# Keys and values of a cached attention block in mixed rows of 65536 bytes, three loads for two heads

## The chip, the core and the metric

The kernel runs on one core of one Trainium2 chip. The metric is the device time of one execution in microseconds (us). Times below are from one profiled execution, unless a median of runs is named. The engines are called PE (matrix products; PEld is its loading of weights), DVE (vector), ACT (activations), POOL and SP (which issues every load here).

## What is computed

One token passes through a transformer block with adaptive normalisation. All numbers are float32. The attention has 32 heads of width 192 and a cache of 8192 keys and values for each head, so the two caches hold 402.7 MB of the 451.8 MB that the kernel reads.

```python
D = 640; H, Sk, Dh = 32, 8192, 192; F = 1536
mod = (silu(c) @ w_mod).reshape(6, D)            # sa, ca, ga, sb, cb, gb
h = layernorm(x) * (1 + ca) + sa
q = (h @ wq).reshape(H, Dh)
scores = einsum("hd,hkd->hk", q, k_cache) * Dh ** -0.5
p = softmax(scores)
o = einsum("hk,hkd->hd", p, v_cache)
x = x + ga * (o.reshape(H * Dh) @ wo)
h = layernorm(x) * (1 + cb) + sb
x = x + gb * (relu(h @ w1 + b1) ** 2 @ w2 + b2)
```

## The kernel before

**Tiles.** A head's 8192 positions lie on 128 partitions, 64 positions each. A head's keys are therefore one tile of 128 rows of 12288 numbers (49152 bytes), and its values another. There are four large buffers: `k0` and `k1` for the keys of even and odd heads, `v0` and `v1` for their values. A row of `k0` or `k1` has room for 1920 more numbers. With 26 of the 32 heads a piece of a weight is appended to the keys: with an even head the columns of `wq` for the next two heads, with an odd head the rows of `wo` for two earlier heads. Such a row has 14208 numbers (56832 bytes).

**One head.** DVE multiplies the keys in place by the query, which lies in `qb` on all partitions (L368). It sums 36 of the 64 positions over the 192 dimensions (L370). For the other 28, POOL first adds the second half of the dimensions to the first (L347), and DVE sums what is left (L376). Then comes the maximum over the positions: DVE in each partition (L378), PE across partitions, DVE again (L380, negated). ACT forms the exponentials (L315) and PE multiplies them with the values: 24 products, which the profile counts as 48 (L271). For two heads together PE forms the next query from `wq` in `k0` (L283).

**Work that lies inside the next pair.** Between L370 and L376 of an even head, DVE divides the two outputs before by their sums and sorts them (L388, L354, L356). Between L370 and L376 of an odd head it multiplies an earlier pair's outputs with the rows of `wo` that came with the keys and adds them to `acc` (L405, three instructions a pair). For the last five pairs `wo` is loaded after the keys (`wot`), and its products stand behind the loop: three pairs on DVE (L468), two on PE (L489).

**Order of the loads.** SP issues all loads by one function (L135) into one queue. It waits for a buffer to come free before each: `tk_f0` and `tk_f1` say that DVE has finished the keys, a mark of PE that the values were used. Behind the last heads come `wot`, `wm1` (second half of `w_mod`), `w1` and `w2` in four pieces, 73 loads in all.

**The end.** After the last values PE turns the outputs (L288), forms the attention's result (L489, L497), then the second normalisation (L508 to L519), the product with `w1` (L529), squares, and the product with `w2` (L548), whose pieces it waits for one by one.

```python
    def dma(dst, src, s):
        nc.sync.dma_start(dst, src).then_inc(s, 16)
```

Of the kernel before, what the change touches and what calls it, by code (L numbers as in the profile page):

```python
# [9 lines left out]
P = 128  # L10
# [16 lines left out]
HALF = NPOS // 2  # L27
FOLD = 7
WO = 3 * D
WQ = KB * PW  # L30
HD = NPOS * DH
KSLOT = HD + WO
NTAIL = 4
WITHOUT_W = (1, H - 2, *range(H + 1 - 2 * NTAIL, H, 2))
WITH_W = tuple(h for h in range(H) if h not in WITHOUT_W)
SMALL = 2 * KB + FB + KB
W0 = KB * 3 * D + WQ + SMALL
W2_CUT = (6 * D, 9 * D, 11 * D, FB * D)
EPS = 1e-5
# [52 lines left out]
def block_kernel(nc, kw, ky, vc, wm0, wot, wm1, w1, w2, out):  # L92
# [4 lines left out]
    k0_sem = sem("k_first")  # L97
    k_sem = [sem(f"k{s}") for s in range(2)]
    b_sem = [sem(f"v{s}") for s in range(2)]
    w_sem = [sem(f"w{n}") for n in range(9)]  # L100
    me, tk_mul, tk_n = sem("me"), sem("tk_mul"), sem("tk_n")
    tk_free = [sem("tk_f0"), sem("tk_f1")]
    tk_fold, tk_qb, tk_v, tk_x, tk_t = sem("tk_fold"), sem("tk_qb"), sem("tk_v"), sem("tk_x"), sem("tk_t")
    tk_q, tk_m, tk_o = sem("tk_q"), sem("tk_m"), sem("tk_o")
# [9 lines left out]

    k_t = [sb(f"k{s}", KSLOT) for s in range(2)]
    v_t = [sb(f"v{s}", HD) for s in range(2)]
# [3 lines left out]
    qb, ga, x_t, bbt = sb("qb", PW), sb("ga", DG), sb("x_t", DG), sb("bbt", 32 * (FB + KB))  # L120
# [4 lines left out]
    sp = sb("sp", 2)  # L125
    r2 = sb("r", 2)
    om, os_ = sb("om", ED, E), sb("os", 2, ED)
    oT, oTs, acc = sb("oT", 1 + NTAIL, NV), sb("oTs", NV), sb("acc", D)
# [8 lines left out]
    dma(v_t[1][:, :W0], wm0, w_sem[0])  # L137

    def keys_of(h):
        return kw[WITH_W.index(h)] if h in WITH_W else ky[WITHOUT_W.index(h)]  # L140
# [15 lines left out]
    pool.memset(eps_t[:, :], EPS)  # L156
    m_quad = L.mark(pool.memset(quad[:, :], 0.0))
# [5 lines left out]
    L.e.wait_ge(*m_set).then_inc(tk_o, 1)  # L163
# [3 lines left out]
    head = v_t[1][:, W0:]  # L167
# [5 lines left out]
    m_small = V.mark(v.tensor_copy(small[:, :], v_t[1][:, W0 - SMALL:W0]))  # L173
# [47 lines left out]
    m_mod = mod(ps_o[0], v_t[1][:, :KB * 3 * D], 3, range(KB))  # L221
# [16 lines left out]
    T.wait(m_h1)  # L238
    wq0 = v_t[1][:, KB * 3 * D:KB * 3 * D + WQ].rearrange("p (b n) -> p b n", b=KB)
    for b in range(KB):  # L240
        i = pe.matmul(ps_q[:, :PW], h1[:, b:b + 1].to_broadcast([P, P]), wq0[:, b], start=(b == 0), stop=(b == KB - 1))
    m_q = T.mark(i)
# [12 lines left out]


    PE_STEPS = ("q", "oT", "v0", "sum", "v1")
# [4 lines left out]
    T0 = T.n  # L262

    def pe_values(s):
        T.take(b_sem[s], 16)
        T.take(tk_p[s])
        t = v_t[s][:, :].rearrange("p (j g n) -> p j g n", g=NV, n=E * ED)
        n = NPOS // E
        for j in range(n):
            for g in range(NV):  # L270
                i = pe.matmul(ps_o[s][32 * g:32 * (g + 1), :], p_t[s][:, E * j:E * (j + 1)].rearrange("p e r -> p (e r)"),  # L271
                              t[:, j, g], start=(j == 0), stop=(j == n - 1))
        i.then_inc(T.sem, 1)
# [16 lines left out]
    def pe_sum():  # L290
# [27 lines left out]
    late, turned_to = NPAIR - 1 - NTAIL, {}
    act_query(0, m_q)
    for i in range(NPAIR):  # L320
        if i:
            A.wait(done("oT", i))
            turned = act.activation(oTs[:, :] if i <= late else oT[:, i - 1 - late], ps_oT[:, :NV], AF.Copy)  # L323
            if i <= late:
                turned.then_inc(tk_t, 1)
            else:
                turned_to[i - 1] = A.mark(turned)
        act_exp(2 * i)
        if i + 1 < NPAIR:
# [28 lines left out]
    def dve_keys(h, between):  # L358
        s = h % 2
        for n, (a, b) in enumerate(parts(h)):  # L360
            if h == 0 and n == 0:
                V.wait((k0_sem, 16))
            else:
                B.take(k_sem[s], 16)
            if s == 0 and n == 0:
                B.take(tk_qb)
            pr, r, keep = keys(s, a, b), sc[s][:, a:b], b - a - FOLD * (b - a) // 16
            B.mark(v.tensor_mul(pr, pr, qb[:, None, DH * s:DH * (s + 1)].to_broadcast([P, b - a, DH])))  # L368
            B.tell(tk_mul)
# [12 lines left out]
    def dve_pair(i, projected, attended):  # L382

        def even():
            if not projected:
                return
# [12 lines left out]
        def odd():  # L399
            if attended:  # L400
                B.take(tk_t)
                w = k_t[1][:, HD:].rearrange("p (j n) -> p j n", j=NV)
                for j in range(NV):
                    B.wait()
                    B.mark(v.scalar_tensor_tensor(acc[:, :], w[:, j], oTs[:, j:j + 1], acc[:, :], op0=ALU.mult, op1=ALU.add))  # L405

        dve_keys(2 * i, even)
        dve_keys(2 * i + 1, odd)
# [3 lines left out]
    dve_pair(0, False, False)  # L412
    for first, end, attended in ((1, late + 1, True), (late + 1, NPAIR, False)):
        with nc.Fori(first, end, engines=bass.OrderedEngineSet([ET.DVE])):
            dve_pair(first, True, attended)


    S.wait(m_q, m_h1, m_ready)
    def load_values(h):
        if h > 1:  # L420
            S.wait(done(f"v{h % 2}", h // 2 - 1))
        dma(v_t[h % 2][:, :], vc[h], b_sem[h % 2])

    def load_keys(h):
        S.wait((tk_free[h % 2], h // 2))
        if h % 2 == 0:
            S.wait(done("q", h // 2 - 1))
        w = KSLOT if h in WITH_W else HD
        dma(k_t[h % 2][:, :w], keys_of(h), k_sem[h % 2])

    for h in range(1, H - 2):
        load_values(h)
        load_keys(h + 1)
# [165 lines left out]
```

## Time and profile before

| what | before |
|---|---|
| median of 3 runs | 1052.62 us (1052.47 to 1052.73) |
| the profiled execution | 1052.46 us |
| its span, first to last instruction | 1051.2 us |
| bytes loaded | 451.8 MB |
| mean rate over the span | 430 GB/s |
| DMA queue's packets, share of 16 engines | 99.6% |
| DVE busy | 852.9 us, 81% |
| PE busy | 412.2 us, 39% |
| POOL busy, ACT busy | 190.1 us, 35.7 us |

The span is 1.26 us shorter than the execution's time. An engine's busy time says only how long it worked. Which resource sets the time is read from the share of the DMA engines, from the waits, and from the chain that ended last.

### The profile page before, as it was taken

How to read it: one execution, taken by the hardware profiler on the slowest of the kernel's cores; microseconds unless marked ns; L12 is line 12 of the kernel's file. 1: busy time of each engine (PE TensorE's matmuls, PEld its weight loads, DVE VectorE, ACT ScalarE, POOL GpSimd, SP SyncE). 2: the span in 40 equal slices, each digit the busy share in tenths (PEclk: the TensorE clock that was granted, in tenths of full speed). 3: DMA queues.
4: the chain of work that ended last, by engine and by line, in shares of the span. 5: the costliest groups of instructions: out<-in, count | busy, mean ns of one | idle time of the engine just before them, and what ended most of it. 6: DMA issues, size and time to landing. Idle time of an engine off the chain costs nothing. (4 is left out here: it accounts for less than half of the span.)

```text
span 1051.2 us, 5316 instructions
## 1 busy us (share of the span) xinstructions
PE 412.2 (39%) x2128; PEld 157.2 (15%) x2128; DVE 852.9 (81%) x327; ACT 35.7 (3%) x103; POOL 190.1 (18%) x48
## 2 busy tenths in 40 slices
PE   2153514344341444424234441433424334353447
PEld 0021201112110111201012110111201111121213
DVE  0976889888889888889888888888889889797983
ACT  1000000000000000000000000000000000000000
POOL 0110222201222210222210222220122222012220
PEclk9676657768566676757767576676756667676669
DMA  9999999999999999999999999999999999999998
GB/s 401 429 451 424 427 430 446 425 436 438 432 428 426 443 441 421 428 445 433 428 434 438 429 428 428 443 438 423 437 434 426 445 428 437 429 428 434 434 427 342
DMA packets 10526, 451.90 MB, mean 430 GB/s; under 512 B 1172, under 2 KB 1176, under 8 KB 1560
## 3 DMA queue, kind: packets, MB, share of 16 engines
q1 hardware_dynamic: 10520, 451.83, 99.6%
q8 instruction: 3, 0.05, 0.0%
q14 instruction: 3, 0.02, 0.0%
HBM read 451.82 MB, written 0.00 MB: 430 GB/s over the span
## 5 line engine op out<-in xcount | busy, mean ns | idle before, releaser
L368 DVE TENSOR_TENSOR k<-k,qb 128x12288 f32<-128x12288 f32 (+1 forms) x33 | 414.8, 12570 | 109.5 <-DVEq L75 109.5
L347 POOL TENSOR_TENSOR k<-k 128x2688 f32<-128x2688 f32 (+1 forms) x33 | 188.1, 5699 | 819.2 <-DVEq L85 819.2
L271 PE MATMUL ps_o<-v,p 128*32 128x512 f32 x1536 | 264.6, 675 | 22.0 <-PEq L57 22.0
L370 DVE TENSOR_REDUCE sc<-k 128x36 f32<-128x6912 f32 (+1 forms) x33 | 235.5, 7135 | 4.8
L283 PE MATMUL ps_q<-k,h 128*128 128x384 f32 x160 | 91.0, 743 | 242.3 <-PEq L57 242.3
L277 PE MATMUL ps_mx<-ident,mp 128*128 128x128 f32 x64 | 19.6, 399 | 326.9 <-PEq L57 326.7
L271 PEld LDWEIGHTS ps_o<-v,p 128*32 128x32 f32 x1536 | 71.5, 122 | 189.4 <-issue 189.1
L376 DVE TENSOR_REDUCE sc<-k 128x28 f32<-128x2688 f32 (+1 forms) x33 | 94.3, 2857 | 0.0
L283 PEld LDWEIGHTS ps_q<-k,h 128*128 128x128 f32 x160 | 46.4, 302 | 290.7 <-issue 287.6
L277 PEld LDWEIGHTS ps_mx<-ident,mp 128*128 128x128 f32 x64 | 12.8, 249 | 341.7 <-issue 341.6
L380 DVE TENSOR_REDUCE nm<-ps_mx 128x1 f32<-128x128 f32 x32 | 9.3, 292 | 33.9 <-DVEq L75 33.9
L405 DVE SCALAR_TENSOR_TENSOR acc<-k,oTs,acc 128x640 f32<-128x640 f32 x33 | 29.1, 882 | 0.8
L315 ACT ACTIVATE p<-sc,nm 128x256 f32<-128x256 f32 x32 | 16.2, 507 | 275.2 <-DVE nm L380 275.2
L354 DVE SCALAR_TENSOR_TENSOR om<-ps_o,r,mask 96x512 f32<-96x512 f32 x32 | 23.9, 746 | 1.1
L356 DVE TENSOR_REDUCE os<-om 96x64 f32<-96x512 f32 x32 | 21.8, 682 | 1.1
L292 PE MATMUL ps_sum<-sp,ones 128*128 128x2 f32 x32 | 8.9, 348 | 20.5 <-PEq L57 20.5
L310 ACT ACTIVATE qb<-ps_q 128x384 f32<-128x384 f32 x16 | 7.9, 491 | 231.6 <-DVEq L85 226.9
L188 PE MATMUL ps_o<-v,silu 128*32 128x480 f32 x40 | 6.4, 804 | 18.4 <-DVE silu L181 18.4
L323 ACT ACTIVATE oTs<-ps_oT 128x3 f32<-128x3 f32 x11 | 1.9, 173 | 328.5 <-PE ps_oT L288 328.5
L292 PEld LDWEIGHTS ps_sum<-sp,ones 128*128 128x128 f32 x32 | 8.0, 311 | 24.8 <-issue 24.8
L173 DVE COPY small<-v 128x27 f32<-128x27 f32 x1 | 0.2, 180 | 14.0 <-DMA v<-in_wm 14.0
L378 DVE TENSOR_REDUCE mp<-sc 128x1 f32<-128x64 f32 x32 | 7.0, 220 | 4.7
(88 smaller groups left out, 84.4 us busy)
## 6 DMA issues: line engine op xcount, KB each, us to landing
v<-in_vc SPq DMA_DIRECT2D x32, 6144.0 KB, 39.4
k<-in_kw SPq DMA_DIRECT2D x25, 7104.0 KB, 35.9
k<-in_ky SPq DMA_DIRECT2D x6, 6144.0 KB, 35.5
v<-in_wm SPq DMA_DIRECT2D x1, 5773.5 KB, 16.6
k<-in_wot SPq DMA_DIRECT2D x1, 4800.0 KB, 28.2
v<-in_wm SPq DMA_DIRECT2D x1, 4800.0 KB, 28.6
k<-in_kw SPq DMA_DIRECT2D x1, 4032.0 KB, 33.3
k<-in_w SPq DMA_DIRECT2D x1, 3840.0 KB, 24.1
```

Source lines behind the costliest of these rows:

```text
L271: i = pe.matmul(ps_o[s][32 * g:32 * (g + 1), :], p_t[s][:, E * j:E * (j + 1)].rearrange("p e r -> p (e r)"), t[:, j, g], start=(j == 0), s ...
L277: pe.matmul(ps_mx[s][:, :P], mp[s][:, :].to_broadcast([P, P]), ident[:, :], start=True, stop=True).then_inc(tk_x, 1)
L283: i = pe.matmul(ps_q[:, :PW], h1[:, b:b + 1].to_broadcast([P, P]), w[:, b], start=(b == 0), stop=(b == KB - 1))
L292: pe.matmul(ps_sum[:, :2], ones[:, :], sp[:, :], start=True, stop=True).then_inc(T.sem, 1)
L315: act.activation(p_t[s][:, :, :], sc[s][:, :, None].to_broadcast([P, NPOS, 32 // E]), AF.Exp, bias=nm[s][:, :], accum_out=sp[:, s:s + 1]). ...
L347: pool.tensor_add(half[:, :, :DH // 2], half[:, :, :DH // 2], half[:, :, DH // 2:]).then_inc(tk_fold, 1)
L354: return (v.scalar_tensor_tensor(om[:n], ps_o[a][:n].rearrange("p (d e) -> p d e", e=E), r2[:n, a:a + 1], mask[:n, None, :].to_broadcast([ ...
L356: lambda: v.tensor_reduce(os_[:n, a], om[:n], axis=AX.X, op=ALU.add))
L368: B.mark(v.tensor_mul(pr, pr, qb[:, None, DH * s:DH * (s + 1)].to_broadcast([P, b - a, DH])))
L370: o = v.tensor_reduce(r[:, :keep], pr[:, :keep], axis=AX.X, op=ALU.add)
L376: B.mark(v.tensor_reduce(r[:, keep:], pr[:, keep:, :DH // 2], axis=AX.X, op=ALU.add))
L405: B.mark(v.scalar_tensor_tensor(acc[:, :], w[:, j], oTs[:, j:j + 1], acc[:, :], op0=ALU.mult, op1=ALU.add))
```

## The change

**Loads.** The four buffers become a ring of three slots of 16384 numbers (65536 bytes) a partition. The first half of a slot holds keys, the second half values. A pair of heads is cut into three chunks. The keys are cut by dimension: dimensions 0 to 127 of the even head; 128 to 191 of the even and 0 to 63 of the odd head; 64 to 191 of the odd head. The values of a pair are cut into three runs of 16 products. Chunk n goes to slot n mod 3, and carries the keys of chunk n and the values of chunk n - 2. There are 48 chunks of keys; loads 48 and 49 (`c48`, `c49`) carry the last values and, in the place of the keys, rows of `wo`.

**Queries.** All of `wq` comes in the first four loads (`l0`, `l1`, `c0`, `c1`). PE computes all queries at once into `qr`, five rounds of up to four pairs (`query_rows`). In the loop ACT picks a pair's row (`act_stage`) and PE copies it to all partitions (`pe_query`, one product instead of five).

**Output weights.** No rows of `wo` come with the keys. They come last: four pairs with `c48`, eight in a load `wos`, four with `c49`. The products of pairs 0 to 13 stand on DVE behind the loop, those of 14 and 15 on PE.

**DVE.** A chunk has one multiplication, two sums and POOL's fold, over 8192 numbers instead of 12288. The two parts of a head's scores are added by one small instruction (L413). SP waits for each landing and passes it on by `tk_k` to DVE and `tk_c` to PE. There are 59 loads.

```diff
-    dma(v_t[1][:, :W0], wm0, w_sem[0])
-    dma(k_t[0][:, :HD // 2], keys_of(0)[:, :HD // 2], k0_sem)
-    dma(k_t[0][:, HD // 2:], keys_of(0)[:, HD // 2:], k_sem[0])
-    dma(k_t[1][:, :HD], keys_of(1), k_sem[1])
-    dma(v_t[0][:, :], vc[0], b_sem[0])
+    dma(slot[2][:, :L0], l0, w_sem[0])
+    dma(slot[1][:, :L1], l1, w_sem[1])
+    dma(slot[0][:, :PART + 4 * WQ], c0, slot_sem[0])
...
+    def dve_keys(s, out, between=None):
+        B.take(tk_k)
+        if s == 0:
+            B.take(tk_qb)
...
+        B.mark(v.tensor_mul(k, k, q))
+        B.tell(tk_mul)
+        v.tensor_reduce(out[:, :keep], r[:, :keep], axis=AX.X, op=ALU.add)
+        if between:
+            between()
+        B.take(tk_fold)
+        B.mark(v.tensor_reduce(out[:, keep:], r[:, keep:, :r.shape[2] // 2], axis=AX.X, op=ALU.add))
+        B.tell(tk_free)
+
+    def dve_max(s, one, two):
+        B.mark(v.tensor_add(sc[s][:, :], one, two))
...
+        dve_keys(0, ra)
+        dve_keys(1, rb, between if projected else None)
+        dve_max(0, ra[:, :], rb[:, :NPOS])
+        dve_keys(2, rc)
+        dve_max(1, rc[:, :], rb[:, NPOS:])
...
+    S.wait(m_w1, m_w2)
+    dma(slot[1][:, :PART + WQ], c1, slot_sem[1])
+    S.wait(m_w0, m_h1, m_ready)
+    dma(slot[2], stream[0], slot_sem[2])
+
+    def forward(n):
+        m = landed(n)
+        if n < PARTS:
+            nc.sync.wait_ge(*m).then_inc(tk_k, 1)
+        if n >= LAG:
+            nc.sync.wait_ge(*m).then_inc(tk_c, 1)
...
+    def issue(n):
+        old = n - 3
+        S.wait((tk_free, old + 1))
+        if old >= LAG:
+            S.wait(values_done(old - LAG))
...
+            dma(slot[n % 3], stream[n - LAG], slot_sem[n % 3])
...
+    forward(0)
+    for n in range(1, PARTS - 1):
+        forward(n)
+        issue(n + 2)
+    forward(PARTS - 1)
+    S.wait((tk_free, PARTS), values_done(PARTS - 3))
+    dma(slot[2][:, :MIDDLE * WO], wos, w_sem[2])
+    issue(PARTS + 1)
+    forward(PARTS)
+    forward(PARTS + 1)
+
+    attend_range(0, EARLY, landed(PARTS))
+    attend_range(EARLY, EARLY + MIDDLE, (w_sem[2], 16))
...
+    S.wait(done("vb", NPAIR - 1), attended[EARLY - 1])
+    dma(wm1_t, wm1, w_sem[3])
+    S.wait(attended[EARLY + 3])
+    dma(w1_t, w1, w_sem[4])
+    S.wait(attended[EARLY + MIDDLE - 1])
...
+        "stream": np.concatenate([kp[LAG:], vp[:-LAG]], axis=2),
+        "c48": join(side(wo, 0, EARLY), vp[-2]),
+        "c49": join(side(wo, EARLY + MIDDLE, 4), vp[-1]),
+        "wos": side(wo, EARLY, MIDDLE),
```

SP's queue at the end of the program, before; `k0` to `v1` are the four buffers, `pe` and `tk_f0`, `tk_f1` the marks that a buffer is free:

```order
L135 DMA v0<-in_vc 128x12288 [waits pe]
L135 DMA v1<-in_vc 128x12288 [waits pe]
L135 DMA k0<-in_wot 128x9600 [waits pe,tk_f0]
L135 DMA v0<-in_wm1 128x9600 [waits pe]
L135 DMA k1<-in_w1 128x7680 [waits tk_f1]
L135 DMA v1<-in_w2 128x3840 [waits pe]
```

Now; `slot0` to `slot2` are the landings of loads to the slots, `tk_free` says that DVE has finished a chunk's keys:

```order
L144 DMA ring<-in_stream 128x16384 [waits slot0,pe,tk_free]
L144 DMA ring<-in_c48 128x15872 [waits slot1,pe,tk_free]
L144 DMA ring<-in_wos 128x15360 [waits slot2,pe,tk_free]
L144 DMA ring<-in_c49 128x15872
L144 DMA ring<-in_wm1 128x9600 [waits slot0,slot1,dve,pe]
L144 DMA ring<-in_w1 128x7680 [waits dve]
L144 DMA ring<-in_w2 128x3840 [waits dve]
```

Before, each of these loads waited for an engine to free its buffer. Now `c48` and `wos` wait for an earlier load's landing as well, and SP's waits ahead of `wm1` are for the landings of `c48` (`slot0`) and `c49` (`slot1`), the load issued just before it.

DVE behind its loop, before; `k0` holds `wot`:

```order
L471 RECIPROCAL r<-ps_sum 128x2 [waits pe]
L354 SCALAR_TENSOR_TENSOR om<-ps_o0,r,mask 96x512 [waits dve]
L356 TENSOR_REDUCE os<-om 96x64 [waits dve]
L468 SCALAR_TENSOR_TENSOR acc<-k0,oT,acc 128x640 [waits act,w8,dve]
L468 SCALAR_TENSOR_TENSOR acc<-k0,oT,acc 128x640 [waits dve] x2
```

Now, the first rows of the 36 products with `wo` there, and the rows that stand behind them:

```order
L451 SCALAR_TENSOR_TENSOR acc<-ring,oT,acc 128x640 [waits act,slot0]
L451 SCALAR_TENSOR_TENSOR acc<-ring,oT,acc 128x640 [waits dve] x2
...
L451 SCALAR_TENSOR_TENSOR acc<-ring,oT,acc 128x640 [waits dve,act,w2]
...
L515 RECIPROCAL r<-ps_sum 128x2 [waits pe]
L388 SCALAR_TENSOR_TENSOR om<-ps_o0,r,mask 96x512 [waits pe,dve]
L390 TENSOR_REDUCE os<-om 96x64 [waits dve]
L451 SCALAR_TENSOR_TENSOR acc<-ring,oT,acc 128x640 [waits act,slot1,dve]
```

Behind the loop there were nine products with `wo` on DVE; now there are 42, of which 36 stand ahead of the division of the last pair's outputs, 24 of them behind the landing of `wos` (`w2`).

## Rows read from the trace of the kernel before

**Rows 1.** The page: span; GB/s in 40 equal slices; DMA packets; the load queue.
```profile
span 1051.2 us, 5316 instructions
GB/s 401 429 451 424 427 430 446 425 436 438 432 428 426 443 441 421 428 445 433 428 434 438 429 428 428 443 438 423 437 434 426 445 428 437 429 428 434 434 427 342
q1 hardware_dynamic: 10520, 451.83, 99.6%
```

**Rows 2.** Stretches A:B: length, busy us by engine, clock, DMA share, GB/s.
```profile
502.60:565.30 62.70, 23.01 (x120) 8.84 (x117) 52.90 (x19) 1.86 (x6) 11.75 (x2) 0.70 1.00 433
...
1017.00:1027.40 10.40, 10.26 (x63) 3.17 (x66) 9.14 (x12) 0.00 (x0) 0.00 (x0) 0.72 0.98 421
...
1031.00:1038.90 7.90, 7.31 (x56) 2.13 (x49) 3.70 (x14) 0.47 (x2) 0.00 (x0) 1.00 0.97 418
```

**Rows 3.** DVE's timeline: multiplications of odd heads' keys (start, us, what, idle before).
```profile
471.42 12.96 DVE L368 TENSOR_TENSOR k<-k,qb 128x12288 f32<-128x12288 f32 x1 [3.76 <-DVEq L75]
...
784.64 12.96 DVE L368 TENSOR_TENSOR k<-k,qb 128x12288 f32<-128x12288 f32 x1 [3.75 <-DVEq L75]
...
845.03 12.96 DVE L368 TENSOR_TENSOR k<-k,qb 128x12288 f32<-128x12288 f32 x1 [6.39 <-DVEq L75]
```

**Rows 4.** Timeline of the launch: first load issued, first instruction that needs it.
```profile
0.75 0.40 SPq L135 DMA_DIRECT2D v<-in_wm  x1
...
17.32 0.18 DVE L173 COPY small<-v 128x27 f32<-128x27 f32 x1 [14.04 <-DMA v<-in_wm]
```

**Rows 5.** Groups of instructions by shape (busy, mean ns of one, idle before).
```profile
L368 DVE TENSOR_TENSOR k<-k,qb 128x12288 f32<-128x12288 f32 x31 | 401.7, 12958 | 108.0 <-DVEq L75 108.0
...
L370 DVE TENSOR_REDUCE sc<-k 128x36 f32<-128x6912 f32 x31 | 228.0, 7353 | 4.5
L347 POOL TENSOR_TENSOR k<-k 128x2688 f32<-128x2688 f32 x31 | 182.0, 5871 | 774.8 <-DVEq L85 774.8
...
L368 DVE TENSOR_TENSOR k<-k,qb 128x6144 f32<-128x6144 f32 x2 | 13.1, 6552 | 1.5 <-DVEq L75 1.5
...
L188 PE MATMUL ps_o<-v,silu 128*32 128x480 f32 x40 | 6.4, 804 | 18.4 <-DVE silu L181 18.4
```

**Rows 6.** DVE's timeline through the end of the last even head.
```profile
976.65 7.35 DVE L370 TENSOR_REDUCE sc<-k 128x36 f32<-128x6912 f32 x1
983.92 0.16 DVE L388 RECIPROCAL r<-ps_sum 128x2 f32<-128x2 f32 x1
...
987.00 2.94 DVE L376 TENSOR_REDUCE sc<-k 128x28 f32<-128x2688 f32 x1
990.08 0.22 DVE L378 TENSOR_REDUCE mp<-sc 128x1 f32<-128x64 f32 x1
991.06 0.29 DVE L380 TENSOR_REDUCE nm<-ps_mx 128x1 f32<-128x128 f32 x1 [0.76 <-DVEq L75]
991.27 12.95 DVE L368 TENSOR_TENSOR k<-k,qb 128x12288 f32<-128x12288 f32 x1
```

**Rows 7.** PE's timeline: one head's values.
```profile
960.74 9.09 PE L271 MATMUL ps_o<-v,p 128*32 128x512 f32 x48
```

**Rows 8.** Timeline of the end, several engines.
```profile
1019.44 8.38 DVE L468 SCALAR_TENSOR_TENSOR acc<-k,oT,acc 128x640 f32<-128x640 f32 x9
...
1028.51 0.68 DVE L356 TENSOR_REDUCE os<-om 96x64 f32<-96x512 f32 x1
...
1031.04 0.33 DVE L508 TENSOR_TENSOR k<-ps_att,ga 128x160 f32<-128x160 f32 x1 [1.85 <-PE ps_att L489]
...
1037.38 0.34 DVE L519 STREAM_TRANSPOSE k<-k 128x160 f32<-128x160 f32 x1
...
1038.92 3.43 PE L529 MATMUL ps_o<-k 128*32 128x384 f32 x40 [0.60 <-DMA k<-in_w]
...
1047.34 1.25 PE L548 MATMUL ps_o<-v,k 128*32 128x160 f32 x24 [0.45 <-DMA v<-in_w]
...
1049.37 0.65 SPq L135 DMA_DIRECT2D out_y<-k  x1
```

More of the change, by code (lines that the diff above doesn't have):

```diff
@@ L89, in close, with block_kernel @@
         self.n = 0
-def block_kernel(nc, kw, ky, vc, wm0, wot, wm1, w1, w2, out):
+def block_kernel(nc, l0, l1, c0, c1, stream, c48, c49, wos, wm1, w1, w2, out):
     sem = nc.alloc_semaphore
@@ new lines, in act_stage, with pe_query @@
+    def act_stage(i):
+        r = [i in pairs for pairs in ROUNDS].index(True)
+        g = ROUNDS[r].index(i)
+        A.wait(m_rows[r])
+        return act.activation(stage[:, :], qr[:, r], AF.Copy, scale=ident[:, 32 * g:32 * g + 1])
+    def pe_query():
+        return pe.matmul(ps_q[:, :PW], ones[:, :], stage[:, :], start=True, stop=True)
+    m_rows = {}
+    A.wait(m_set)
+    m_w0 = query_rows(0, slot[2][:, KB * 3 * D:], ps_att)
+    m_rows[0] = keep_rows(0, ps_att, m_w0)
+    T.wait(A.mark(act_stage(0)))
@@ L424, in load_keys @@
[L424 to L433, printed above, removed]
-    load_keys(H - 1)
-    load_values(H - 2)
-    load_values(H - 1)
-    wot_t, wm1_t, w1_t, w2_t = k_t[0], v_t[0], k_t[1], v_t[1]
-    S.wait((tk_free[0], NPAIR), done("q", NPAIR - 1))
@@ L441, in block_kernel, with attend @@
-    dma(wot_t[:, :(1 + NTAIL) * WO], wot, w_sem[8])
-    S.wait(done("v0", NPAIR - 1))
-    dma(wm1_t[:, :KB * 3 * D], wm1, w_sem[1])
-    S.wait((tk_free[1], NPAIR))
-    dma(w1_t[:, :KB * FF], w1, w_sem[2])
-    S.wait(done("v1", NPAIR - 1))
+    dve_pair(False)
+    with nc.Fori(1, NPAIR, engines=bass.OrderedEngineSet([ET.DVE])):
+        dve_pair(True)
+    def attend(i, w, m):
+        w = w.rearrange("p (j n) -> p j n", j=NV)
+        V.wait(m, turned[i])
+        for j in range(NV):
+            V.wait(V.last())
+            V.mark(v.scalar_tensor_tensor(acc[:, :], w[:, j], oT[:, i, j:j + 1], acc[:, :], op0=ALU.mult, op1=ALU.add))
+        return V.last()
@@ new lines, in block_kernel, with late_wo, attend_range @@
+    WO_AT = PART - 4 * WO
+    def late_wo(i):
+        if i < EARLY:
+            at = slot[0], WO_AT + i * WO
+        elif i < EARLY + MIDDLE:
+            at = slot[2], (i - EARLY) * WO
+        else:
+            at = slot[1], WO_AT + (i - EARLY - MIDDLE) * WO
+        return at[0][:, at[1]:at[1] + WO]
+    attended = {}
+    def attend_range(first, end, m):
+        for i in range(first, end):
+            attended[i] = attend(i, late_wo(i), m)
+    S.wait(m_w1, m_w2)
+    dma(slot[1][:, :PART + WQ], c1, slot_sem[1])
@@ new lines, in block_kernel @@
+    forward(0)
[10 more added lines that the diff above has]
+    attend_range(EARLY, EARLY + MIDDLE, (w_sem[2], 16))
+    V.wait(done("sum", NPAIR - 1))
+    V.wait(V.mark(v.reciprocal(r2[:, :], ps_sum[:, :2])))
+    for a in range(2):
+        V.wait(done("vb" if a == 0 else "vc", NPAIR - 1))
+        scaled, sums = project(a)
+        V.wait(V.mark(scaled))
+        o = sums()
+        if a == 0:
+            V.wait(V.mark(o))
+            attend_range(EARLY + MIDDLE, ON_DVE, landed(PARTS + 1))
+        else:
+            o.then_inc(tk_o, 1)
```

339 lines of the change are left out of this document (163 added, 176 removed).

## The prediction

> **What bounds the kernel now.** I read the page first: the load queue takes 99.6% of the span of all 16 DMA engines [rows 1]. No slice but the first and the last falls under 421 GB/s. Then the table of stretches: DMA share 1.00, while DVE is busy for 52.9 us of 62.7 [rows 2]. Then DVE's own rows. A multiplication of keys starts 3.8 or 6.4 us late, because its keys have not landed [rows 3]. Loading is the bound from the launch to the last piece of `w2`, and each engine only keeps pace. So two things count: what the queue needs for the same bytes, and each moment in which it has nothing to do.
>
> **What a load costs in the full queue.** The bytes follow from the code, the times from [rows 3]. From 471.42 to 784.64 lie five pairs with 27.13 MB each: 62.644 us a pair. From 784.64 to 845.03 lie four loads with 26.15 MB: 60.39 us. The difference, 0.983 MB in 2.254 us, is 436 GB/s. At that rate 27.13 MB need 62.2 us, so four loads cost 0.43 us beside their bytes, 0.1 us each. As the steps are read to 0.01 us, 0.06 to 0.11 is possible. The bytes stay; 73 loads become 59. **Term 1: 14 x 0.1 = -1.4 at most and -0.8 at least; I take -1.0.** That is all there is to gain, since the queue never ran dry. The SBUF page of the Trainium skill ("SBUF — State Buffer", The DMA setup-cost knee) gives each transfer a fixed cost of about 2 us. By it the sum would get -28 us here; in the full queue the trace disagrees, with 0.1 us.
>
> **What a load costs in an empty queue.** The launch shows it: SP issues the first load at 0.75, and DVE uses it at 17.32 [rows 4]. Its 5.91 MB need 13.6 us at 436 GB/s. The other 2.9 us are the price of the start. The lower bound is the output's store: issued at 1049.37 [rows 8], over at the span's end, 1051.2 [rows 1], so 1.8 us. A load into an empty queue therefore lands 1.8 to 2.9 us late; I take 2.9, as the launch is the same kind of load.
>
> **The loop.** A full chunk is 8.39 MB: 19.35 us. When chunk n lands, SP issues chunk n + 2, provided that DVE and PE are done with chunk n - 1, while chunk n + 1 is on its way. The queue runs dry only if that comes 18 us late. DVE per chunk: the multiplication goes by 6552 ns for 6144 and 12958 for 12288 numbers [rows 5], so 8.69 us for 8192; handover 0.14; the sum over 4608 numbers at 7353 ns for 6912, 4.95; the last sum, two thirds of 2.94 [rows 6], 2.0. Together 15.7. POOL's fold, two thirds of 5.87 [rows 5], 3.9 us, hides beside the 4.95. The second chunk also has the division of the outputs, 983.92 to 987.00, 3.1 us, and two chunks have the maximum, 990.08 to 991.27 [rows 6], with the added instruction (0.22 and a handover) 1.6. A pair: 3 x 15.7 + 3.1 + 3.2 = 53.4 us, against 58.05 of loading. PE's 16 products of a chunk are two thirds of 9.09 [rows 7], 6 us, well inside a chunk. The products with `wo` leave the loop. The query's five products become one, and so does ACT's part grow by one row: both beside the loading. Worth nothing, as long as the 4.6 us of slack stand.
>
> **The start.** Three loads (23.9 MB, 55 us) are queued at once. `c1` is issued after `l1` has landed (40 us) and two rounds of queries are done (a round is at most 40 products of 384 columns; 40 of 480 take 6.4 us [rows 5], so under 13). The queue ends at 58.5. Worth nothing, with 5 us to spare.
>
> **The first gap, `wos`.** SP waits until DVE has finished chunk 47. Let T be that chunk's landing. Chunk 46 landed at T - 19.35; DVE needs 15.7 + 3.1 + 1.6 and 0.2 for tokens, and starts on chunk 47 at T + 1.3. It is done at T + 17.0. `c48` (8.13 MB) keeps the queue busy until T + 18.7. If the queue counts as empty, `wos` lands at T + 17.1 + 2.9 + its 18.1; if not, at T + 18.7 + 18.1. **Term 2: 0 to 1.3; I take 0.8**, as part of the 2.9 is spent before the queue is dry.
>
> **The second gap, `wm1`.** SP issues `c49`, waits until `c49` itself has landed (it has to tell PE), and only then issues `wm1`. Nothing else is queued. The next two loads, `w1` and `w2`, stand behind `wm1` on SP. **Term 3: 0.1 for SP's waits and 1.8 to 2.9 for the start; I take 2.9.**
>
> **The end.** It is hidden by the last loads. From `wos` to `w1` the loads need 18.7 + 2.9 + 11.4 + 9.1 = 42.1 us. In that time DVE makes 24 products with `wo` at 8.38 / 9 [rows 8], 22.3 us; divides a head, 1.5; makes six more, 5.6; divides the other, 1.5. Then 1.85 us to L508 (1029.19 to 1031.04) and 6.7 to the end of L519 [rows 8]. Together 39.5 us: 2.6 less than the loads. From the landing of `w1` on, the loads and the work are those of before, where PE waits for the last piece of `w2` [rows 8]. The products moved out of the loop cost nothing then; without this cover, each us over 2.6 would show.
>
> **Sum.** 1052.46 - 1.0 + 0.8 + 2.9 = 1055.2 us, by the profiled execution's own time, which is 0.16 below the median. Bounds: -1.4 + 0 + 1.9 gives 1053.0, -0.8 + 1.3 + 3.0 gives 1056.0. The measurement tells about 0.2% from no change, 2.1 us: up to 1054.7 counts as no change. I forecast slightly slower.
>
> **Rivals.**
> - *Starting again is cheap; not slower.* `wm1` pays 1.8 + 0.1 as the store did, and `wos` reaches the queue before it is dry. Then 1052.46 - 1.0 + 1.9 = 1053.4. It decides if both gaps together cost under 3.1 us. For it: DVE's finish and the end of `c48` lie within 1.7 us, and the launch may have paid for more than the load. Against: the store moves 2.5 KB and the launch is the nearer row.
> - *The end overtakes the loads.* PE ran at a granted clock of 0.72 while warming up on the last values, and at 1.00 in the end [rows 2], its levels being 1.2 and 2.4 GHz. It now pauses for 2 to 3 us between the last values and the end. At the lower level its share of the 6.7 us, the 3.43 of L529 and the products of L548 would double: 2 to 10 us more, about 1060.
> - *A row of 65536 bytes is no single packet.* 10520 packets [rows 1] are 73 loads of 128 rows and 16 closing ones, and 8 of the output: each row is one packet, up to 56832 bytes. No longer row is shown. If each were two, 46 loads would pay their 0.06 to 0.1 once more: 1058 to 1060.
> - *Rows that begin 65536 bytes apart load more slowly.* The rows of 49152 and 56832 bytes lie on one line to 0.1 us a load, which speaks against it. At 421 instead of 433 GB/s [rows 1, 2], 46 x 19.35 = 890 us would become 915: 1080. The Trainium skill warns of it ("DMA: Bandwidth & Descriptors", Latency and other measured facts): a row pitch of 512 KiB gave 207 GB/s instead of 214. By that ratio the sum would grow by 29 us. No run here has such a pitch.
> - *Each load pays its start.* With 2.9 us a load, 14 fewer would give 1012. But 73 such loads would have left the queue idle for 210 us, and it was full [rows 1]. The setup-cost rule named above would give 1027.
> - *DVE becomes the bound*, if rows of 64 numbers cost it 9% more than rows of 192. Each us over 58.05 a pair counts 16 times.
>
> **How the numbers follow.** Forecast 0.47; cheap start 0.27; late end 0.09; two packets 0.07; slow rows 0.04; DVE 0.04; each load its start 0.02. About 0.08 of the forecast lies under 1054.7. Slower by over 0.2%: 0.39 + 0.09 + 0.07 + 0.04 + 0.04, less 0.01 = 0.62. Within: 0.27 + 0.08 = 0.35. Faster: 0.03. The range from 1052.8 to 1059.5 holds the forecast, the cheap start, half of the late end and most of the two packets.
>
> **What would show it.** In the profile of the changed kernel: 59 x 144 + 8 = 8504 packets; DMA share 1.00 in the loop, with 58.05 us for a pair and some 4 us of DVE waiting for keys; SP's issue of `wos` 17 us behind the landing of chunk 47; `wm1` issued with an empty queue, landing 14.3 us later instead of 11.4; at the end PE waiting for `w2`. I am wrong if the loop's pair is not 58.05 us, if DVE does not wait for chunks, or if L508 comes after `w1`.

## The result and the profile after

The changed kernel takes 1057.01 us (median of 6 runs, 1056.65 to 1057.43). The kernel before, run beside it, takes 1052.66. The ratio is 1.0042, with a 95% interval of 1.0029 to 1.0054: slower by 0.4%, 4.35 us. The profiled execution took 1057.43 us, with a span of 1056.1; against the profiled execution before, that is 4.97 us more. The forecast was slower by 2.7 us.

The page of the kernel after (span; GB/s in 40 slices; three DMA queues with packets, MB and share of 16 engines; a group of instructions; two DMA issues with KB and us to landing), which answers to [rows 1] and [rows 5]:

```profile
span 1056.1 us, 5657 instructions
...
GB/s 410 422 444 420 435 434 437 437 434 437 437 437 432 432 422 430 434 434 437 437 435 437 437 427 432 434 427 429 437 434 437 434 437 437 432 429 440 382 377 339
...
q1 hardware_dynamic: 8504, 451.83, 99.1%
q8 instruction: 4, 0.07, 0.0%
q14 instruction: 5, 0.04, 0.0%
...
L403 DVE TENSOR_TENSOR ring<-ring,qb 128x8192 f32<-128x8192 f32 x48 | 417.1, 8689 | 85.0 <-DVEq L85 84.9
...
ring<-in_wos SPq DMA_DIRECT2D x1, 7680.0 KB, 20.9
...
ring<-in_wm SPq DMA_DIRECT2D x1, 4800.0 KB, 15.2
```

Read the load queue `q1` first. It was idle for 0.9% of 1056.1 us, 9.5 us, against 0.4% of 1051.2, 4.2 us, before. The difference, 5.3 us, is about the size of the loss (the shares are rounded to 0.1%, or 1 us), and the slices tell where it lies: no slice in the loop falls under 420 GB/s, where the lowest before had 421, but the 38th and the 39th, each 26.4 us long, have 382 and 377 GB/s where before they had 434 and 427.

Stretches of the kernel after (columns as in [rows 2]): a pair of heads in the loop, and the surroundings of the two dips:

```profile
502.60:560.65 58.05, 25.95 (x109) 7.71 (x106) 51.02 (x21) 2.37 (x7) 11.87 (x3) 0.68 1.00 433
976.00:979.00 3.00, 0.00 (x0) 0.00 (x0) 3.00 (x2) 0.00 (x0) 0.67 (x1) 0.50 0.69 296
...
1018.00:1021.00 3.00, 1.48 (x6) 0.45 (x9) 2.82 (x4) 0.00 (x0) 0.00 (x0) 0.50 0.70 192
1021.00:1034.00 13.00, 8.73 (x83) 4.01 (x81) 10.26 (x14) 1.46 (x2) 0.00 (x0) 0.76 0.92 395
```

The loop runs at DMA share 1.00 and 433 GB/s, as before. The share falls to 0.69 and 0.70 around two issues. SP's timeline of the kernel after shows them:

```profile
943.23 0.33 SPq L144 DMA_DIRECT2D ring<-in_c  x1
979.68 0.33 SPq L144 DMA_DIRECT2D ring<-in_wos  x1
980.05 0.43 SPq L144 DMA_DIRECT2D ring<-in_c  x1
1019.48 0.33 SPq L144 DMA_DIRECT2D ring<-in_wm  x1
1019.86 5.12 SPq L144 DMA_DIRECT2D ring<-in_w  x5
1054.34 0.66 SPq L144 DMA_DIRECT2D out_y<-ring  x1
```

Between `c48` at 943.23 and `wos` at 979.68 SP issues nothing for 36.5 us; between `c49` at 980.05 and `wm1` at 1019.48, nothing for 39.4 us. In both cases two loads or more were queued at the start of that time. At its end the queue was empty, or held no more than the last rows of one load.

**The loss, landing by landing.** A load's 128 rows lie on the 16 DMA engines, and the trace holds the time at which each engine finished its part. From these 16 records per load the following is worked out. "Step" is the time since the last engine's landing of the load before, and "spread" the time from the first engine's landing to the last's. The fourth column is the step of a load of the same size in a full queue.

| load | last engine | step | at the full queue's rate | spread |
|---|---|---|---|---|
| chunk 47 | 962.37 | 19.35 | 19.35 | 2.35 |
| `c48` | 981.12 | 18.75 | 18.75 | 2.35 |
| `wos` | 1000.62 | 19.50 | 18.13 | 0.97 |
| `c49` | 1019.35 | 18.73 | 18.75 | 0.97 |
| `wm1` | 1034.66 | 15.31 | 11.37 | 1.89 |
| last of `w2` | 1053.04 | | | |

The first gap costs 1.37 us, the second 3.94. The last piece of `w2` landed at 1048.07 before and at 1053.04 after: 4.97 us, the whole difference. What is left over, 4.97 - 1.37 - 3.94 = -0.34, is what everything else brought, the fewer loads among it.

The timeline of the end of the kernel after answers to [rows 8]:

```profile
1000.64 22.53 DVE L451 SCALAR_TENSOR_TENSOR acc<-ring,oT,acc 128x640 f32<-128x640 f32 x24 [7.77 <-DMA ring<-in_wos]
...
1030.26 0.74 DVE L388 SCALAR_TENSOR_TENSOR om<-ps_o,r,mask 96x512 f32<-96x512 f32 x1
1030.40 0.76 PE L565 MATMUL ps_att<-acc,ones 128*32 128x160 f32 x8 [3.31 <-DVE acc L451]
...
1034.58 0.33 DVE L572 TENSOR_TENSOR ring<-ps_att,ga 128x160 f32<-128x160 f32 x1 [2.86 <-PE ps_att L556]
...
1041.90 0.35 DVE L583 STREAM_TRANSPOSE ring<-ring 128x160 f32<-128x160 f32 x1
...
1043.91 3.43 PE L593 MATMUL ps_o<-ring 128*32 128x384 f32 x40 [1.08 <-DMA ring<-in_w]
...
1052.33 1.24 PE L612 MATMUL ps_o<-ring 128*32 128x160 f32 x24 [0.45 <-DMA ring<-in_w]
```

PE still waits for `w1` at 1043.91 (L593, L529 before) and for the last piece of `w2` at 1052.33 (L612, L548 before). The end is hidden, and everything behind the second gap is late by what the loads are late.

Stretches of the kernel after, from the last sum to L572 and from there to the end of L583:

```profile
1031.70:1034.60 2.90, 2.39 (x26) 1.49 (x26) 0.04 (x2) 1.46 (x2) 0.00 (x0) 0.50 0.89 382
1034.60:1042.30 7.70, 7.59 (x56) 2.33 (x56) 2.87 (x12) 0.26 (x1) 0.00 (x0) 0.90 0.99 425
```

The same two of the kernel before, to L508 and to the end of L519:

```profile
1029.20:1031.00 1.80, 1.40 (x30) 1.23 (x34) 0.00 (x0) 1.25 (x2) 0.00 (x0) 1.00 0.91 393
1031.00:1037.80 6.80, 6.79 (x56) 2.13 (x48) 2.91 (x12) 0.47 (x2) 0.00 (x0) 1.00 0.97 416
```

### The profile page after: what moved, and what is told of

The parts are those of the page before. It is cut to its first block, busy times and chain, and to the rows that moved or that the text cites. A ratio compares the mean times of both kernels' runs of the same rounds, so it can differ in the third digit from the quotient of the medians.

```text
span 1056.1 us, 5657 instructions
## 1 busy us (share of the span) xinstructions
PE 465.0 (44%) x2152; PEld 142.3 (13%) x2152; DVE 865.3 (82%) x404; ACT 46.3 (4%) x124; POOL 193.6 (18%) x64
## 3 DMA queue, kind: packets, MB, share of 16 engines
q1 hardware_dynamic: 8504, 451.83, 99.1%
## 5 line engine op out<-in xcount | busy, mean ns | idle before, releaser
L403 DVE TENSOR_TENSOR ring<-ring,qb 128x8192 f32<-128x8192 f32 x48 | 417.1, 8689 | 85.0 <-DVEq L85 84.9
L313 PE MATMUL ps_o<-ring,p 128*32 128x512 f32 x1536 | 360.0, 816 | 202.8 <-PEq L67 202.8
L381 POOL TENSOR_TENSOR ring<-ring 128x1792 f32<-128x1792 f32 x48 | 189.8, 3955 | 782.2 <-DVEq L95 782.2
L313 PEld LDWEIGHTS ps_o<-ring,p 128*32 128x32 f32 x1536 | 86.9, 143 | 451.7 <-issue 451.4
L405 DVE TENSOR_REDUCE rc<-ring 128x36 f32<-128x4608 f32 x16 | 79.2, 4953 | 2.3
L405 DVE TENSOR_REDUCE rb<-ring 128x72 f32<-128x4608 f32 x16 | 79.3, 4953 | 2.3
L405 DVE TENSOR_REDUCE ra<-ring 128x36 f32<-128x4608 f32 x16 | 79.2, 4953 | 2.3
L451 DVE SCALAR_TENSOR_TENSOR acc<-ring,oT,acc 128x640 f32<-128x640 f32 x42 | 37.1, 884 | 10.0 <-DMA ring<-in_wos 7.8
L409 DVE TENSOR_REDUCE ra<-ring 128x28 f32<-128x1792 f32 x16 | 32.1, 2009 | 0.0
L409 DVE TENSOR_REDUCE rc<-ring 128x28 f32<-128x1792 f32 x16 | 32.1, 2009 | 0.0
L390 DVE TENSOR_REDUCE os<-om 96x64 f32<-96x512 f32 x32 | 21.8, 682 | 1.1
## 6 DMA issues: line engine op xcount, KB each, us to landing
ring<-in_wm SPq DMA_DIRECT2D x1, 4800.0 KB, 15.2
```

The costliest lines, as they stand in the source:

```text
L313: i = pe.matmul(ps_o[h][32 * g:32 * (g + 1), :], p_t[h][:, E * j:E * (j + 1)].rearrange("p e r -> p (e r)"), t[:, k], start=(j == 0), stop ...
L381: pool.tensor_add(r[:, keep:, :w], r[:, keep:, :w], r[:, keep:, w:]).then_inc(tk_fold, 1)
L390: lambda: v.tensor_reduce(os_[:n, a], om[:n], axis=AX.X, op=ALU.add))
L403: B.mark(v.tensor_mul(k, k, q))
L405: v.tensor_reduce(out[:, :keep], r[:, :keep], axis=AX.X, op=ALU.add)
L409: B.mark(v.tensor_reduce(out[:, keep:], r[:, keep:, :r.shape[2] // 2], axis=AX.X, op=ALU.add))
```

## Experiments

All times are medians. The kernel before, beside each of them, had a median of 1052.63 to 1052.81. The theory at this point: the two gaps are the whole loss, the first 1.4 us and the second 3.0, the price of starting in an empty queue. The rival: something in the stream itself (longer rows, their pitch, fewer loads, DVE) costs as much.

### Taking the gaps away

*One gap fewer: `wm1` ahead of the last landing.* SP's wait for `c49` is moved behind the issue of `wm1`, whose buffer is long free by then.

```diff
     forward(PARTS)
-    forward(PARTS + 1)
...
     dma(wm1_t, wm1, w_sem[3])
+    forward(PARTS + 1)
```

> The changed kernel with one line moved: SP issues wm1 before it waits for the landing of c49, so the second gap of the queue goes. Theory (a load into the empty queue lands 2.9 us late, and SP's waits take 0.1): 3.0 us less than the changed kernel's 1057.0, so 1054.0. The profile of the changed kernel has wm1 15.3 us behind c49 by the last engine instead of 11.4, which would give 1053.1. Rival 'starting again is cheap' (1.9 us): 1055.1. Rival 'the end's work is the bound, not the loads': no change, 1057.0.

Measured: 1054.99 us (1054.18 to 1056.04), ratio 1.0021 [1.0012, 1.0030]. That is 2.0 less than the changed kernel, 1.0 less than the theory's 3.0, and next to the 1055.1 of cheap starts. The traces tell the two apart. The last piece of `w2` lands at 1049.63 instead of 1053.04, so the loads have gained 3.41 us, and `wm1` lands 12.29 us behind `c49` instead of 15.31: there the gap had cost 3.0, as the theory says. But the output's store is issued 3.08 us behind the landing of the last piece of `w2`, where it is 1.30 us in the kernel before and in the changed one. PE's timeline of this kernel:

```profile
1042.79 3.76 PE L593 MATMUL ps_o<-ring 128*32 128x384 f32 x40
...
1048.46 3.47 PE L612 MATMUL ps_o<-ring 128*32 128x160 f32 x96 [1.91 <-DVE ring L602]
```

`w1` had landed at 1040.35, and all 96 products with `w2` wait for DVE, none of them for a load. With the second gap closed and the first still open, the work of the end is the bound, and 1.78 us of what the loads gain are lost in it. The rival of the end's work was right in that part.

*The other gap: `wos` in two loads.* The half of the slot that held values is free 7.6 us before DVE is done with the keys in the other half; four pairs' rows of `wo` go there at once, and DVE takes these pairs first.

```diff
-    S.wait((tk_free, PARTS), values_done(PARTS - 3))
-    dma(slot[2][:, :MIDDLE * WO], wos, w_sem[2])
+    S.wait(values_done(PARTS - 3))
+    dma(slot[2][:, PART:PART + 4 * WO], wos[:, 4 * WO:], w_sem[10])
+    S.wait((tk_free, PARTS))
+    dma(slot[2][:, :4 * WO], wos[:, :4 * WO], w_sem[2])
...
-    attend_range(EARLY, EARLY + MIDDLE, (w_sem[2], 16))
+    attend_range(EARLY + 4, EARLY + MIDDLE, (w_sem[10], 16))
+    attend_range(EARLY, EARLY + 4, (w_sem[2], 16))
```

> The changed kernel with wos cut into two loads of four pairs: the first goes to the values' half of slot 2, which is free some 6 us after va, the second to the keys' half as before. DVE takes the pairs in the order of landing. The first gap goes, the second stays. Theory: 1.4 us less, one more load 0.1 more: 1055.7. Rival (the queue was not dry there, the time went elsewhere): no change, 1057.0 to 1057.1.

Measured: 1055.86 us (1055.44 to 1056.66), ratio 1.0030 [1.0017, 1.0042], 1.15 less than the changed kernel.

*Both edits together:*

> Both edits together. Theory: the gaps are the whole loss, and what is left is the gain of 13 loads at 0.06 to 0.1 us: 1051.4 to 1052.0 by the mean of the engines, up to 1052.7 if the slowest engine decides (it has 0.8 us more behind it in the changed kernel). Rival (rows 65536 bytes apart, or the products with wo at the end, cost something of their own): above 1053.5.

Measured: 1052.24 us (1051.75 to 1052.42), ratio 0.9995 [0.9986, 1.0004]. Both edits take 4.77 us off, and the difference to the kernel before is gone. The page's queue and the stretches where the dips were:

```profile
q1 hardware_dynamic: 8648, 451.83, 99.5%
```

```profile
976.00:979.00 3.00, 0.00 (x0) 0.00 (x0) 3.00 (x2) 0.00 (x0) 0.88 (x1) 0.50 0.95 409
...
1018.00:1034.00 16.00, 14.27 (x130) 5.72 (x134) 8.04 (x14) 1.72 (x3) 0.00 (x0) 0.85 1.00 429
```

The share is 0.95 where it was 0.69, and 1.00 where it was 0.70 and 0.92. So the two gaps are the loss; everything else in the change, taken together, makes no difference that can be measured. But the gaps don't add. Alone, the first costs 2.75 (1054.99 - 1052.24) and the second 3.62 (1055.86 - 1052.24), 6.37 in all; together they cost 4.77, 1.6 us less. The landings show where most of that goes. In the four profiled executions the last piece of `w2` lands at 1053.04 with both gaps, at 1049.63 with the first alone, at 1051.69 with the second alone and at 1048.04 with none. For the loads the gaps therefore cost 1.59 and 3.65 alone and 5.00 together, only 0.24 less than their sum. The store is issued 1.30 us behind that landing in three of the four kernels, and 3.08 us behind it with the first gap alone. The 1.78 us between are the work of the end, which shows only there. (In these executions the shortfall is 2.0 us; the one with the first gap alone is 0.8 above its median.)

### What one start costs

*The queue is drained eight more times.* In the changed kernel SP waits, before eight of the loads of the loop, until the load before has landed.

```diff
             S.wait(m_w4)
+        if n in (9, 13, 17, 21, 25, 29, 33, 37):
+            S.wait(landed(n - 1))
         if n < PARTS:
```

> The changed kernel, and at eight of the 46 loads of the stream SP first waits for the landing of the load before it, so that the queue runs dry eight times more. It measures the price of a start alone. Theory (2.9 us for the start and 0.1 for the waits): 8 x 3.0 = 24 us more, 1081. Rival (the store's 1.8 and 0.1): 8 x 1.9 = 15 us more, 1072. In the profile the stretch of a pair with a drain takes 61 us instead of 58.05.

Measured: 1077.95 us (1077.44 to 1078.2), ratio 1.0239 [1.0223, 1.0254]: 20.94 more than the changed kernel, 2.6 for each drain, between what the two theories gave. The stretches around one of them, the drain, the start and the full queue again:

```profile
187.00:207.00 20.00, 7.53 (x34) 2.25 (x34) 18.27 (x8) 0.17 (x1) 3.92 (x1) 0.67 0.87 377
207.00:212.00 5.00, 2.77 (x11) 1.16 (x14) 3.75 (x5) 0.60 (x2) 0.00 (x0) 0.50 0.95 354
212.00:229.00 17.00, 8.34 (x32) 2.65 (x26) 13.44 (x6) 1.59 (x4) 3.98 (x1) 0.70 1.01 439
```

A drained load's last landing comes 21.8 to 22.0 us after the one before, where the others take 19.35: about 2.5 us for SP's wait and the start. The theory's 3.0 was too dear for them, and the rival's 1.9 too cheap.

*One drain, without the gaps.* The same wait, ahead of load 41 alone, in the kernel with both edits.

```diff
+        if n == 41:
+            S.wait(landed(n - 1))
```

> The kernel with both gaps closed (1052.24), and one start from an empty queue far from the end: SP waits for the landing of load 40 before it issues load 41, some 170 us ahead of the end. Closing one gap of the changed kernel won 1.15 or 2.0 us, closing both 4.8: some 1.6 us are paid once by whichever gap is there. Theory (a start lines the 16 engines up, and each later load of instructions then makes its engine the last): 2.5 for the start and about 1 for those loads, 1055.7 or more. Rival (the 1.6 us belong to the place, the end of the program): 2.5 alone, 1054.7.

Measured: 1055.66 us (1055.34 to 1056.69), ratio 1.0028 [1.0017, 1.0040], 3.42 more than without it. The run was made to explain the 1.6 us above, which are mostly the end's work; what it shows stands by itself. (SP issues load 41 some 228 us ahead of the end, not 170.) The drained load's step is 21.84 instead of 19.35, which is 2.5. Most of the rest appears some 185 us later: `wm1` takes 12.66 from `c49`, where without the drain it takes 11.38. (The profiled execution is 0.9 us above the median, so these steps add up to more than 3.42.) The landings show why. Without the drain the engines arrive at `wm1` with a spread of 2.52 us and leave it with 2.54. With the drain they had been lined up (the spread fell from 2.64 to 0.58), and at `wm1` one of them falls behind, from a spread of 0.39 to 1.64. The mean of the 16 engines moves by 11.5 us in both. So in both kernels little happens to the engines as a whole, and one engine loses 1.3 us or more; that shows only where this engine is not ahead of the others. At that time both traces have a load of instructions, a packet of 16384 bytes that takes 0.98 us (1.02 without the drain). The one packet of the load queue that starts within 0.02 us of its end takes 0.55 us longer than its like (0.54), together 1.5 us.

*The same gap in the kernel before.* SP waits for `wot` before it issues `wm1`.

```diff
-    S.wait(done("v0", NPAIR - 1))
+    S.wait(done("v0", NPAIR - 1), (w_sem[8], 16))
     dma(wm1_t[:, :KB * 3 * D], wm1, w_sem[1])
```

> The kernel before, with one wait more: SP issues wm1 only when the load ahead of it (wot) has landed, so that its full queue runs dry once. Theory: the start costs 2.5 us as in the eight drains, 1055.2; and since a start lines the 16 engines up again, the program's own load of instructions at 1028 us, which takes about 1.4 us of one engine, makes that engine the last: 1 us more, 1056.2. Rival (the price belongs to the changed kernel's end alone): no change, 1052.7. Rival (store's price): 1054.6.

Measured: 1056.52 us (1056.01 to 1057.08), ratio 1.0037 [1.0023, 1.0050], 3.9 more. DMA issues (KB, us to landing) and SP's timeline of this kernel:

```profile
v<-in_wm SPq DMA_DIRECT2D x1, 4800.0 KB, 14.9
```

```profile
1018.34 0.33 SPq L135 DMA_DIRECT2D v<-in_wm  x1
```

The load lands 14.9 us after its issue, where its bytes need 11.4. One waiting line on SP, with buffers, loads and order all as before, does nearly the whole harm of the change. Here too more than the start is paid: `wm1` lands 3.38 us later behind `wot` than without the wait.

### The stream

*Each load of the stream in two halves.* The 46 loads of 65536 bytes a row become 92 of 32768, in the kernel with both edits.

```diff
-            dma(slot[n % 3], stream[n - LAG], slot_sem[n % 3])
+            dma(slot[n % 3][:, :PART], stream[n - LAG][:, :PART], slot_sem[n % 3])
+            dma(slot[n % 3][:, PART:], stream[n - LAG][:, PART:], slot_sem[n % 3])
```

> The kernel with both gaps closed (1052.24), and each of the 46 loads of the stream cut into two, keys and values apart: 46 loads and 5888 packets more in a queue that stays full. It measures what a load, with its eight rows for each engine, costs beside its bytes. Theory (0.06 to 0.11 us): 2.8 to 5.1 us more, 1055.0 to 1057.3. Rival 'each load pays its start' (2.5 us by the eight drains): 115 us more, 1167. Rival (rows of 65536 bytes load more slowly than shorter ones): less than 2.8 more, or faster.

Measured: 1055.76 us (1055.39 to 1055.84), ratio 1.0029 [1.0017, 1.0040], 3.5 more for 46 more loads: 0.076 us each. The queue on its page:

```profile
q1 hardware_dynamic: 15272, 451.83, 99.6%
```

It is as full as ever. A load in a full queue costs 0.08 us, far from the 2.5 of one in an empty queue. The Trainium skill's fixed cost of about 2 us for each transfer ("SBUF — State Buffer", The DMA setup-cost knee) is therefore no price of a load as such here; it comes near what a start in an empty queue takes. The halves land every 9.714 us, two of them in 19.43 instead of 19.35. Rows half as long load no faster, so the length of the row costs nothing here. The pitch of 65536 bytes is the same in both kernels; that it costs nothing is read from the loop of the changed kernel, which runs at the same 433 GB/s as the rows of 49152 and 56832 bytes before.

*More work on DVE.* In the kernel with both edits DVE makes four products of 640 numbers into a scratch tile in each pair, between the two sums of the third chunk, 3.64 us; then nine, 8.24 us.

```diff
+        def more():
+            for _ in range(4):
+                B.wait()
+                B.mark(v.scalar_tensor_tensor(dum[:, :], dum[:, :], ident[:, :1], dum[:, :], op0=ALU.mult, op1=ALU.add))
-        dve_keys(2, rc)
+        dve_keys(2, rc, more)
```

> The kernel with both gaps closed, and DVE makes four more products of 640 numbers on a scratch tile in each pair, 0.93 us each, 3.7 us a pair. The trace of the changed kernel has 3.95 us a pair in which DVE waits for keys. Theory (the loads are the bound of the loop): no change, 1052.2. Rival (DVE is the bound somewhere in the loop): each us of a pair counts up to 16 times, up to 1111.

> The same with nine products, 8.4 us a pair, 4.4 more than DVE waits. Theory: DVE becomes the bound, and 15 or 16 pairs pay 4.4 us each: 66 to 71 us more, 1118 to 1123, with the queue running dry once DVE is some 17 us behind. Rival (the slack is larger than the waits shown): clearly less.

Measured: with four 1058.73 us (1057.65 to 1059.2), ratio 1.0054 [1.0040, 1.0067], 6.5 more than without them; with nine 1128.84 (2 runs), ratio 1.0724 [1.0704, 1.0743], 76.6 more. Both expectations were too low: the first said no change, the second 66 to 71 us. DVE's timeline in the loop of the changed kernel (multiplications, idle time ahead in brackets), and a pair's stretch with the four products:

```profile
517.56 8.69 DVE L403 TENSOR_TENSOR ring<-ring,qb 128x8192 f32<-128x8192 f32 x1 [0.42 <-DVEq L85]
536.80 8.69 DVE L403 TENSOR_TENSOR ring<-ring,qb 128x8192 f32<-128x8192 f32 x1 [3.53 <-DVEq L85]
557.49 8.68 DVE L403 TENSOR_TENSOR ring<-ring,qb 128x8192 f32<-128x8192 f32 x1
```

```profile
502.60:561.06 58.46, 25.28 (x107) 7.71 (x108) 54.48 (x24) 2.37 (x7) 11.87 (x3) 0.68 1.00 433
```

DVE waits 0.42 + 3.53 = 3.95 us a pair, and 3.64 more work should have fitted. But with it a pair takes 58.46 us, and two of the three multiplications still start 0.56 and 0.26 us late, though their keys landed some 8 and 5 us before. Those 0.8 us are handovers, not slack. The slack is 58.05 - (58.46 - 3.64) = 3.2 us. DVE then loses 0.4 us a pair, and the loads of the loop don't feel it (share 1.00): DVE only falls behind, some 6 us over the loop, within the lead that the buffers allow. It shows behind the loop, in SP's and PE's timelines of this kernel:

```profile
979.26 11.63 SPq L145 DMA_DIRECT2D ring<-in_wos  x2
...
1045.79 3.76 PE L603 MATMUL ps_o<-ring 128*32 128x384 f32 x40
...
1051.45 3.47 PE L622 MATMUL ps_o<-ring 128*32 128x160 f32 x96 [1.91 <-DVE ring L612]
```

SP can issue the second half of `wos` only at 990.57, when DVE is done with the keys; the first half lands at 990.93, so the queue runs dry again. The two halves take 9.90 and 11.31 us instead of 9.11 each, and the last piece of `w2` lands at 1051.70 instead of 1048.04, 3.7 us later. On top of that PE waits for DVE, and no longer for `w1` and `w2`: the end has overtaken the loads, and the store is issued 4.0 us behind that landing instead of 1.3, another 2.7. With nine products the loop itself is bound by DVE, whose multiplications come 62.86 us apart:

```profile
560.29 8.69 DVE L405 TENSOR_TENSOR ring<-ring,qb 128x8192 f32<-128x8192 f32 x1 [0.34 <-DVEq L85]
...
623.15 8.69 DVE L405 TENSOR_TENSOR ring<-ring,qb 128x8192 f32<-128x8192 f32 x1 [0.34 <-DVEq L85]
```

62.86 - 58.05 = 4.8, times 16 pairs 77, as measured. The expectation counted 4.4 a pair, as it took all of the waiting for slack.

## Why the prediction was right in kind and short in size

- **What bounds the kernel.** Right: the loads, before and after. In the profiled executions the changed kernel ends later by exactly what its last load lands later.
- **Term 1, fewer loads: -1.0.** The price of a load was right: 0.06 to 0.11 predicted, 0.076 shown by the stream in halves. But only -0.34 is left at the last engine. By the landings, one engine falls behind by 1.45 us at `c0`, near 44 us, when a load of instructions runs; in the kernel before such a moment, near 32 us, costs the last engine 0.7. That these are the missing 0.7 us is read from the landings alone; no run moved them.
- **The start's price: 1.8 to 2.9, taken 2.9.** The drains show 2.5, with SP's wait in it, and closing the second gap alone 3.0 at `wm1`. The launch [rows 4] was the right neighbour, by the drains a little too dear (its rows give 17.32 - 0.75 - 13.6 = 3.0 rather than 2.9); the output's store [rows 8] too cheap.
- **The loop.** A pair takes 58.05 us, as worked out, and nothing of it shows. DVE's 53.4 us a pair were short by 1.2 to 1.4: with four and nine products the pair less their time is 54.8 and 54.6. The step counted too little for handovers: 0.14 a chunk, where the trace with four products has 0.56 and 0.26 more in a pair ahead of the multiplications alone. The 4.6 us of slack are 3.2, which sufficed. (By the rows named, the first sum of a chunk is 4.90 us, not 4.95; it took 4.95.)
- **Term 2, the first gap: 0.8 of 0 to 1.3.** SP's issue was predicted at T + 17.1, with T the landing of chunk 47, and `c48` at T + 18.7; they came at T + 17.3 and T + 18.75. The step that failed is that part of the start would be hidden. `wos` lands 20.94 us after its issue by the chain of waits, 18.13 + 2.8: the full price. The gap is 1.37 at the last engine, just over the upper bound; at the mean of the engines, most of which were done with `c48` before, it is 2.4.
- **Term 3, the second gap: 0.1 + 2.9.** SP's part was right: `c49` lands at 1019.35, `wm1` is issued at 1019.48. The load was to take 14.3 us from its issue instead of 11.4, and took 15.2; its step is 3.94 over the full queue's. Closing this gap alone took 3.0 of that away at `wm1` (15.31 to 12.29), as forecast; by the drains a start is 2.5. The other 0.9 to 1.4 are the engine that falls behind in the middle of `wm1`, which the single drain showed at the same place, 12.66 instead of 11.38. A start costs its 2.5 to 3 us and lines the engines up; after that, the next thing that holds up one engine holds up the end. This second part isn't in the prediction at all: it took the start for the whole price.
- **The end, hidden with 2.6 us to spare.** Right that it is hidden. The spare time is 1.5: L583 ends at 1042.25 and `w1` lands at 1043.78. PE had waited 3.31 us for DVE ahead of L565, and from the last sum to L572 its granted clock was 0.50, the lower level of 1.2 GHz, where before it was 1.00, 2.4 GHz. L572 comes 2.87 us after the last sum, where L508 came 1.85 after [rows 8]. From there to the transposition it is 7.67, not 6.7, at a clock of 0.90; in this stretch PE also has the first products with `wm1`, which landed only at 1034.66. The late end that was named as a rival did happen, with 2 us, the least of the 2 to 10 it gave, and inside its cover. The cover was worth what the prediction says of it: with the second gap alone closed the loads came 3.41 us sooner, and the end's work took back 1.78, near the 1.9 that 3.41 is over the spare 1.5.
- **The rivals.** Cheap starts are refuted by the drains (2.5 us, not 1.8 + 0.1) and by both gaps together, which cost 4.8 us where the rival needed under 3.1; the 1054.99 next to their 1055.1 came about by the end's work. Two packets for a row of 65536 bytes: the queue has 8504 packets, 59 x 144 + 8. Rows 65536 bytes apart: 433 GB/s in the loop, as before; the Trainium skill's loss at a pitch of 512 KiB ("DMA: Bandwidth & Descriptors", Latency and other measured facts) has no counterpart at 64 KiB here, and the larger pitch wasn't tried. A start for each load: 0.076 us, not 2.9. DVE as the bound: not in the change, but the price of 16 for each microsecond a pair holds, as the nine products showed.
- **The sum.** Predicted -1.0 + 0.8 + 2.9 = 2.7; the 0.1 for SP's waits stands in term 3 and in the bounds, but not in the sum. Found in the profiled execution: -0.34 + 1.37 + 3.94 = 4.97, and 4.35 by the medians. The forecast, slightly slower by dried queues, was the mechanism; each term was off by 0.6 to 1.0 us in the same direction. In the first and the third the reason is, by the landings, that the last of 16 DMA engines decides and not their mean; in the second a start that was thought half hidden wasn't.
- **Luck in the range.** The bounds of the sum end at 1056.0, and 1057.01 lies outside them. It lies inside the range, up to 1059.5, because of the room that was kept for a late end and for two packets a row, neither of which added to the time.

What stays open: that the engine falls behind because it loads instructions. No run took such a load away. The packets' records speak for it. In the changed kernel, apart from the first packets of the three starts (the launch, `wos` and `wm1`), only nine packets of the load queue take over 0.25 us longer than the median of their size, by 0.28 to 0.57. Each of the nine starts within 0.02 us of the end of one of the nine loads of instructions. At 44 us the load of instructions takes 1.01 us and the packet behind it 0.47 more, together 1.47, and the last landing of `c0` is the 1.45 late.

## What to carry to other kernels

Where loads are the bound, look through the issuing queue for every wait for a landing, or for work on the newest data, that stands ahead of another load with nothing else queued: each such place costs a start, here 2.5 to 3 us, while a load more in a full queue costs 0.08. Cutting a load so that its first half needs only what is free early, or moving a wait behind the next issue, gives that time back, as far as the work behind the loads keeps up: moving the wait alone won 2.0 us where the loads gained 3.4. And an engine's idle time is not all slack: only adding work shows how much fits.

## What the runs showed beyond that

- A row of 65536 bytes goes as one packet, of 2422 ns, and a load of 128 such rows takes 19.35 us.
- The 16 DMA engines run up to 2.7 us apart for a whole execution, and keep that distance through hundreds of packets. A start in an empty queue brings them within 0.4 to 1.2 us.
- The page counts loads of instructions, nine with 0.11 MB together, too little to see in any mean. Where the engine that a load of instructions falls on is among the last, a load's last landing comes up to 1.5 us late (1.45 near 44 us in the changed kernel); where it is ahead, nothing shows (near 84 us a step of 19.36).
- One drain that takes 2.5 us out of the load queue cost 3.4 us in the end; eight of them, in a kernel with two gaps already, cost 2.6 each.
